# Input loads as one sequence on one queue, and the bias sums moved between tile transposes

## The chip, the cores and the metric

The kernel runs on one core of a Trainium2 chip. A core has five engines that run side by side, each through its own list of instructions: TensorE (PE in the profile; its weight loads are listed as PEld), VectorE (DVE), ScalarE (ACT), GpSimd (POOL) and SyncE (SP). They wait for each other through semaphores. SP, ACT and POOL also issue transfers (DMAs), each on its own queue, which 16 DMA engines carry out. The metric is the device time of the program in microseconds (us), as the median of several runs.

## The reference

The kernel computes six cross layers of a recommendation model, all in bf16, with a batch of 4096 rows and a width of 26 x 16 = 416 columns:

```python
x = x0                                # 4096 x 416
for l in range(6):
    x = x0 * (x @ ws[l] + bs[l]) + x  # ws[l]: 416 x 416, bs[l]: 416
return x
```

## The kernel before

The activations are held transposed, with features on the 128 partitions and batch rows along the free axis. The 416 features are three blocks of 128 (NC = 3) and a tail of 32. The batch is worked on in four strips of 1024 rows, and each strip in two halves of 512. The sum over the layers stays in PSUM, the memory that matmuls write: a bank is never cleared between the layers of a strip, so it holds the sum of all the products so far. Adding the sums of the biases so far and multiplying by x0 then gives the next layer's input. These bias sums are themselves a matmul: `bsa_sb` holds a row of ones and the six bias rows, `u_sb` is a triangle of ones, and the product lands in bank 1 and is copied to `cb_sb`.

Most matmuls are "column tiles": four of them (`tile_mm`, line 265), each with a 128 x 32 weight, write four groups of 32 partitions side by side. We call four such matmuls a group. The tail rows of the weights (`wt_sb`, `wc_sb`) are used by matmuls of 32 weight rows and 128 columns (lines 393 and 409).

**Steady work.** In layer n, PE does the first half's three output blocks (36 matmuls), then the tail rows, then the tail columns (12 matmuls) and the second half (36). When the tail rows are done (semaphore `s_ti`), DVE works through six `scalar_tensor_tensor` operations (line 537), three for each half; the next layer's tail rows wait for the last of them (`s_xb`). ACT and POOL handle the 32 tail features.

**The start.** Before anything else, PE runs 40 fill matmuls on a constant (line 130), whose results are not used. Rows 0-767 of the first strip are loaded as they are (`xin_sb`: rows 256-511, 0-255 and 512-767 are three transfers of 208 KB) and transposed on PE. Rows 768-1023 come by a DMA transpose (line 158), which SP issues after rows 0-255 have landed. W0 is the first layer's main weight, 312 KB. `xtl_sb` is the tail of rows 768-1023, read in pieces of 64 bytes.

PE's order is: the fill; the bias sums (16 matmuls, weights of 7 rows); four more fill matmuls; the transposes of rows 256-511 and then of rows 0-255, each as six full 128 x 128 transposes (line 312); then the first layer. Its first half is computed block by block of the inner dimension (k = 0, 1, 2). Inside k = 2, PE waits for rows 512-767 and xtl, and does the tail inputs and `third_input`, which transposes rows 512-767 as ordinary column-tile matmuls with an identity. The second half waits for the DMA transpose (`pe.wait_ge(s_x0T[0], 16)`, line 422).

DVE first copies the bias sums (line 506) and then the transposed blocks c = 0 and 2 to SBUF (line 512), while ACT copies c = 1 (line 561). The first matmul of the first layer waits for W0 and for three DVE copies (`s_inD`). The copies of the third input are on lines 517 (DVE) and 578 (ACT); line 576 is ACT's copy of the tail inputs. The order of everything is written out by hand.

Of the kernel before, what the change touches and what calls it, by code (L numbers as in the profile page):

```python
# [11 lines left out]
def bass_standalone__dcn_v2_cross__recsys_kernel(  # L12
# [20 lines left out]
    with ExitStack() as es:  # L33
        def sb(name, shape, dt=BF16):
            return es.enter_context(nc.sbuf_tensor(name, shape, dt))
# [20 lines left out]
        ones_sb = sb("ones_sb", [128, 256])  # L56
        bsa_sb = sb("bsa_sb", [L + 1, D])
        u_sb = sb("u_sb", [L + 1, L])
        cb_sb = sb("cb_sb", [128, NC + 1, L], FP32)
# [31 lines left out]
        def wmain(l):  # L91
            return ws[l, 0:DF, :].rearrange("(k p) n -> p k n", p=128)
# [35 lines left out]

        for q in range(4 * 10):
            nc.tensor.matmul(  # L130
                ps[lane(q % 4), 7, 0:256], lhsT=CONST[:, 0:32], rhs=CONST, start=True, stop=True,
                skip_group_check=True, tile_position=(0, 32 * (q % 4)),
            )
        nc.sync.dma_start(bsa_sb[1:L + 1, :], bs[:, :]).then_inc(s_bs, 16)
        nc.sync.dma_start(xin_sb[:, 0:2, :], x0_w[:, 0, :, :]).then_inc(s_xin[0], 16)
        nc.sync.dma_start(xin_sb[:, 4:6, :], x0_w[:, 2, :, :]).then_inc(s_xin[2], 16)
        nc.scalar.dma_start(xin_sb[:, 2:4, :], x0_w[:, 1, :, :]).then_inc(s_xin[1], 16)  # L137
        nc.scalar.dma_start(w_sb[:, 0, :, :], wmain(0)).then_inc(s_w[0], 16)
        nc.scalar.dma_start(xtl_sb[:, :, :], x0_v[:, 6:JS, DF:D]).then_inc(s_xtl0, 16)
        nc.gpsimd.memset(ones_sb[:, :], 1.0).then_inc(s_ones, 1)  # L140
        nc.vector.memset(wc_sb[:, :, :], 0.0).then_inc(s_zero, 1)
        nc.vector.memset(bsa_sb[0:1, :], 1.0).then_inc(s_zero, 1)

# [59 lines left out]
        def _(pool):  # L203
            def load_wc(i, g):
# [10 lines left out]
            pool.affine_select(  # L215
                out=u_sb[:, :], in_=ones_sb[0:L + 1, 0:L], pattern=[[1, L]],
                compare_op=ALU.is_ge, fill=0.0, base=1, channel_multiplier=-1,
            ).then_inc(s_set, 1)
            for g in (0, 2):
                load_wt(pool, g, 0, 1, s_wtp)  # L220
            pool.wait_ge(s_zero, 1)
            for i in range(2):
# [40 lines left out]
        def _(pe):  # L263
            def tile_mm(dst, lhsT, rhs, q, start):
                return pe.matmul(  # L265
                    dst, lhsT=lhsT, rhs=rhs, start=start, stop=True,
                    skip_group_check=True, tile_position=(0, 32 * q),
                )

            def fill(n):  # L270
                for i in range(n):
                    for q in range(4):
                        tile_mm(ps[lane(q), 7, 0:256], CONST[:, 0:32], CONST, q, True)

# [9 lines left out]
            def third_input():  # L284
                pe.wait_ge(s_inD, 4)
                for c in range(NC):
                    for j in range(2):
                        for q in range(4):
                            f0 = c * 128 + 32 * q
                            ins = tile_mm(  # L290
                                ps[lane(q), THIRD[c], j * 128:j * 128 + 128], xin_sb[:, 4 + j, f0:f0 + 32], ident[:, :], q, True
                            )
                    ins.then_inc(s_inT, 1)
# [10 lines left out]

            bias_sums()
            fill(1)
            pe.wait_ge(s_set, 1)
            for i, (h, c) in enumerate(IN_ORDER):
                if c == 0:
                    pe.wait_ge(s_xin[h], 16)  # L310
                for j in range(2 * h, 2 * h + 2):
                    ins = pe.transpose(
                        out=psT[:, IN_BANKS[h][c], (j % 2) * 128:(j % 2 + 1) * 128],
                        in_=xin_sb[:, j, c * 128:(c + 1) * 128], identity=ident[:, :],
                    )
                ins.then_inc(s_inT, 1)
# [187 lines left out]
        def _(dve):  # L504
            dve.wait_ge(s_cbp, 1)
            dve.tensor_copy(
                out=cb_sb[:, :, :], in_=ps[:, 1, 0:8 * (NC + 1)].rearrange("p (c e) -> p c e", e=8)[:, :, 0:L],
            ).then_inc(s_cb, 1)
            for i, (h, c) in enumerate(IN_ORDER):
                if c != 1:  # L510
                    dve.wait_ge(s_inT, i + 1)
                    dve.tensor_copy(
                        out=x0T_sb[:, c, h * 256:(h + 1) * 256], in_=psT[:, IN_BANKS[h][c], 0:256]
                    ).then_inc(s_inD, 1)
            for c in (0, 2):
                dve.wait_ge(s_inT, 2 * NC + c + 1)
                dve.tensor_copy(out=x0T_sb[:, c, 512:768], in_=ps[:, THIRD[c], 0:G]).then_inc(s_inD, 1)
            dve.wait_ge(s_cb, 1)
# [37 lines left out]
        def _(act):  # L556
# [20 lines left out]
            act.wait_ge(s_inT, 2 * NC + 2)  # L577
            act.activation(out=x0T_sb[:, 1, 512:768], in_=ps[:, THIRD[1], 0:G], func=ACTF.Copy).then_inc(s_inA, 1)
            act.wait_ge(s_cb, 1)
# [79 lines left out]
```

## Time and profile before

| what | us |
|---|---|
| median of 6 runs | 128.28 |
| lowest and highest | 128.07, 129.05 |
| the profiled execution | 128.11 |
| its span | 126.9 |
| PE busy | 123.0 (97% of the span) |
| DVE busy | 99.8 (79%) |
| ACT busy | 67.5 (53%) |
| POOL busy | 24.0 (19%) |

The span is the time from the first instruction to the last as the profiler records it; the run's own time is 1.2 us longer. A line of the profile names the source line, the engine, the operation, and "out<-in" with the shapes. `SPq`, `ACTq` and `POOLq` are the issues of transfers by those engines, not the transfers themselves. A `const` in a matmul is the constant of the fill.

The ends of matmuls are modelled and overlap, so a busy PE is not a PE at its peak. A wait in brackets behind a group is the idle time of its engine just before it, and what ended that time.

### The profile page before, as it was taken

What the parts mean: (1) busy time and instruction counts of PE and PEld (TensorE: products, weight loads), DVE (VectorE), ACT (ScalarE), POOL (GpSimd) and SP (SyncE); (2) the same over time, 40 slices, a digit from 0 to 9 for tenths busy, and PEclk for the clock granted to TensorE, in tenths of its full rate; (3) what the DMA queues carried; (4) which work ended last, traced back from release to release, by engine and by line L of the source; (5) the groups of instructions that cost most, each with busy time, mean ns of one, the idle gap of its engine ahead of it and who ended that gap; (6) DMA issues with size and microseconds to landing.
All of it is one profiled execution on the core that took longest, in us unless ns stands there. A gap on an engine that the chain in (4) does not pass through costs nothing.

```text
span 126.9 us, 5323 instructions
## 1 busy us (share of the span) xinstructions
PE 123.0 (97%) x2410; PEld 62.2 (49%) x2410; DVE 99.8 (79%) x154; ACT 67.5 (53%) x146; POOL 24.0 (19%) x44
## 2 busy tenths in 40 slices
PE   7899999999999999999999999999999999999991
PEld 5554544444444445445445445445454454454660
DVE  2359779779779779789788797797797797797973
ACT  0646357377726456475744564574762573566830
POOL 7512202202102013012022023022021021120450
PEclk9999999999999999999999999999999999999999
DMA  3962599400009999700007689940008910530006
GB/s 114 258 144 60 135 280 225 111 0 0 5 3 125 164 140 214 273 4 5 5 0 142 132 161 218 376 123 0 5 0 47 192 40 0 169 105 5 0 31 243
DMA packets 31889, 13.49 MB, mean 106 GB/s; under 512 B 24950, under 2 KB 31868, under 8 KB 31868
## 3 DMA queue, kind: packets, MB, share of 16 engines
q1 hardware_dynamic: 30476, 12.12, 44.9%
q10 hardware_dynamic: 1200, 0.99, 2.5%
q8 instruction: 19, 0.31, 1.0%
q0 software_dynamic: 192, 0.06, 0.4%
q14 instruction: 2, 0.02, 0.0%
HBM read 3.86 MB, written 3.41 MB: 57 GB/s over the span
## 4 chain that ended last, share of the span: by engine, by line
PE 94%; DMA 3%; DVE 0%; ACTq 0%; issue 0%
PE ps L265 81%; PE ps L393 10%; DMA w_sb<-in_ws_dram 3%; PE ps L449 2%; PE ps L464 1%; DVE o_sb L550 0%; PE ps L488 0%; ACTq L137 0%; PE ps L409 0%; PE ps L494 0%
## 5 line engine op out<-in xcount | busy, mean ns | idle before, releaser
L537 DVE SCALAR_TENSOR_TENSOR xT_sb<-ps,cb_sb,x0T_sb 128x512 bf16<-128x512 f32 x120 | 81.0, 744 | 16.5 <-PE ps L393 16.4
L265 PE MATMUL ps<-xT_sb,w_sb 128*32 128x512 bf16 (+1 forms) x1596 | 84.2, 364 | 0.0
L265 PEld LDWEIGHTS ps<-xT_sb,w_sb 128*32 128x32 bf16 x1596 | 41.1, 97 | 37.1 <-issue 4.0
L566 ACT ACTIVATE xt_sb<-xt_sb 32x256 bf16<-32x256 bf16 x76 | 31.5, 414 | 15.7 <-POOL xt_sb L242 15.1
L595 ACT ACTIVATE t_sb<-ps,cb_sb 64x256 f32<-64x256 f32 x46 | 21.5, 468 | 31.3 <-PE ps L265 31.0
L242 POOL TENSOR_TENSOR xt_sb<-t_sb,x0t_sb 128x256 bf16<-128x256 f32 x20 | 13.4, 672 | 81.5 <-ACT t_sb L595 81.5
L265 PE MATMUL ps<-x0T_sb,w_sb 128*32 128x512 bf16 (+1 forms) x336 | 18.5, 365 | 0.4 <-DMA w_sb<-in_ws_dram 0.3
L537 DVE SCALAR_TENSOR_TENSOR xo_sb<-ps,cb_sb,x0T_sb 128x512 bf16<-128x512 f32 x18 | 12.1, 745 | 2.5 <-PE ps L393 2.5
L265 PEld LDWEIGHTS ps<-x0T_sb,w_sb 128*32 128x32 bf16 x336 | 8.6, 97 | 7.9 <-issue 0.6
L393 PE MATMUL ps<-xt_sb,wt_sb 32*128 32x512 bf16 x76 | 11.6, 380 | 0.0
L614 ACT ACTIVATE x0t_sb<-x_sb 32x512 bf16<-32x512 bf16 x12 | 7.5, 626 | 0.3
L409 PE MATMUL ps<-xt_sb,wt_sb 32*128 32x512 bf16 x38 | 7.4, 386 | 0.0
L393 PE MATMUL ps<-xt_sb,wc_sb 32*128 32x256 bf16 x76 | 7.3, 268 | 0.0
L393 PEld LDWEIGHTS ps<-xt_sb,wt_sb 32*128 32x128 bf16 x76 | 2.2, 92 | 8.1 <-DVE xT_sb L537 8.1
L393 PEld LDWEIGHTS ps<-xt_sb,wc_sb 32*128 32x128 bf16 x76 | 3.8, 94 | 2.2
L242 POOL TENSOR_TENSOR xot_sb<-t_sb,x0t_sb 128x256 bf16<-128x256 f32 x3 | 2.0, 672 | 12.6 <-ACT t_sb L595 12.6
L550 DVE SCALAR_TENSOR_TENSOR o_sb<-ps,x0n_sb 128x416 bf16<-128x416 f32 x6 | 3.3, 586 | 1.0 <-PE ps L494 0.9
L570 ACT ACTIVATE xo_sb<-ps,cq_sb 128x512 bf16<-128x512 f32 x5 | 3.3, 686 | 1.1 <-PE ps L393 1.1
L130 PE MATMUL ps<-const-bfloat16-1.0 128*32 128x256 bf16 x40 | 2.3, 418 | 0.8 <-PEq L644 0.8
L561 ACT ACT_TABLE_LOAD x1 | 1.3, 1283 | 3.3 <-issue 3.3
L449 PE MATMUL ps<-w_sb,xT_sb 128*128 128x416 bf16 x12 | 2.8, 341 | 0.0
L265 PE MATMUL ps<-w_sb,xT_sb 128*32 128x416 bf16 x48 | 2.6, 339 | 0.0
(52 smaller groups left out, 38.8 us busy)
## 6 DMA issues: line engine op xcount, KB each, us to landing
out_dram<-o_sb SPq DMA_DIRECT2D x2, 832.0 KB, 4.8
w_sb<-in_ws_dram SPq DMA_DIRECT2D x5, 312.0 KB, 3.9
x0n_sb<-in_x_dram SPq DMA_DIRECT2D x1, 832.0 KB, 5.4
out_dram<-o_sb SPq DMA_DIRECT2D x1, 624.0 KB, 3.7
out_dram<-o_sb SPq DMA_DIRECT2D x3, 208.0 KB, 2.0
xin_sb<-in_x_dram SPq DMA_DIRECT2D x2, 208.0 KB, 3.2
out_dram<-o_sb ACTq DMA_DIRECT2D x2, 208.0 KB, 2.0
w_sb<-in_ws_dram ACTq DMA_DIRECT2D x1, 312.0 KB, 3.7
```

Source lines behind the costliest of these rows:

```text
L130: nc.tensor.matmul(ps[lane(q % 4), 7, 0:256], lhsT=CONST[:, 0:32], rhs=CONST, start=True, stop=True, skip_group_check=True, tile_position= ...
L242: pool.tensor_tensor(out=dst, in0=t32_sb[:, n % 2, :], in1=x0t_sb[:, s, 0:G], op=ALU.mult).then_inc(s_xt, 1)
L265: return pe.matmul(dst, lhsT=lhsT, rhs=rhs, start=start, stop=True, skip_group_check=True, tile_position=(0, 32 * q),)
L393: return pe.matmul(dst, lhsT=lhsT, rhs=srct[lane(g), cols], start=l == 0 and start, stop=True, skip_group_check=True, tile_position=(32 * ...
L409: pe.matmul(ps[:, NC * h + 2, :], lhsT=wt_sb[lane(g), l, 0:128], rhs=srct[lane(g), :].rearrange("p (b r) -> p b r", b=2)[:, ::-1, :], star ...
L449: pe.matmul(ps[:, NAT_BANKS[t], 0:D], lhsT=xT_sb[:, (L - 1) % 2, k, rows], rhs=w_sb[:, L - 1, k, :], start=False, stop=True, skip_group_ch ...
L537: dve.scalar_tensor_tensor(out=dst, in0=ps[:, NC * half + c, :], scalar=cb_sb[:, c, l:l + 1], in1=x0T_sb[:, c, o:o + H], op0=ALU.add, op1= ...
L550: dve.scalar_tensor_tensor(out=o_sb[:, j0 + t, :], in0=ps[:, NAT_BANKS[t], 0:D], scalar=1.0, in1=x0n_sb[:, t, :], op0=ALU.add, op1=ALU.mul ...
L566: ins = act.activation(out=buf[lane(g), G:2 * G], in_=buf[lane(g ^ 1), 0:G], func=ACTF.Copy)
L570: act.activation(out=xo_sb[:, NS - 1, c, half * H:(half + 1) * H], in_=ps[:, NC * half + c, :], func=ACTF.Identity, bias=cq_sb[:, c:c + 1] ...
L595: ins = act.activation(out=t32_sb[HALVES[h], n % 2, :], in_=tail(h), func=ACTF.Identity, bias=cb_sb[HALVES[h], NC, l:l + 1],)
L614: ins = act.activation(out=x0t_sb[lane(g), s + 1, :].rearrange("p (b n) -> p b n", b=2), in_=src[:, ::-1, :] if g % 2 else src, func=ACTF. ...
```

## The change

The four large input loads move to SP's queue, in the order rows 256-511, rows 0-255, W0, rows 512-767. Before, rows 256-511 and W0 were on ACT's queue. The bias load moves from SP's queue to ACT's. There it waits for a memset, because `bsa_sb` now has 128 rows, which are first cleared and then get the row of ones; `u_sb` has 128 rows too. The memset of `wc_sb` now comes third, and POOL's wait for it counts to 3.

On PE, the fill has 48 matmuls instead of 40, and the four extra fill matmuls behind the bias sums are gone. All transposes of rows 0-767 are column-tile transposes of 32 columns each, and `third_input` writes bf16 instead of fp32. The bias sums are computed with 128 rows, between the transposes of rows 256-511 and those of rows 0-255. DVE's copy of the sums moves behind its first two copies.

```diff
-        bsa_sb = sb("bsa_sb", [L + 1, D])
-        u_sb = sb("u_sb", [L + 1, L])
+        bsa_sb = sb("bsa_sb", [128, D])
+        u_sb = sb("u_sb", [128, L])
...
-        for q in range(4 * 10):
+        for q in range(4 * 12):
...
-        nc.sync.dma_start(bsa_sb[1:L + 1, :], bs[:, :]).then_inc(s_bs, 16)
+        nc.sync.dma_start(xin_sb[:, 2:4, :], x0_w[:, 1, :, :]).then_inc(s_xin[1], 16)
         nc.sync.dma_start(xin_sb[:, 0:2, :], x0_w[:, 0, :, :]).then_inc(s_xin[0], 16)
+        nc.sync.dma_start(w_sb[:, 0, :, :], wmain(0)).then_inc(s_w[0], 16)
         nc.sync.dma_start(xin_sb[:, 4:6, :], x0_w[:, 2, :, :]).then_inc(s_xin[2], 16)
-        nc.scalar.dma_start(xin_sb[:, 2:4, :], x0_w[:, 1, :, :]).then_inc(s_xin[1], 16)
-        nc.scalar.dma_start(w_sb[:, 0, :, :], wmain(0)).then_inc(s_w[0], 16)
+        nc.scalar.wait_ge(s_zero, 1)
+        nc.scalar.dma_start(bsa_sb[1:L + 1, :], bs[:, :]).then_inc(s_bs, 16)
         nc.scalar.dma_start(xtl_sb[:, :, :], x0_v[:, 6:JS, DF:D]).then_inc(s_xtl0, 16)
         nc.gpsimd.memset(ones_sb[:, :], 1.0).then_inc(s_ones, 1)
+        nc.vector.memset(bsa_sb[:, :], 0.0).then_inc(s_zero, 1)
+        nc.vector.wait_ge(s_zero, 1)
+        nc.vector.memset(bsa_sb[0:1, :], 1.0).then_inc(s_zero, 1)
         nc.vector.memset(wc_sb[:, :, :], 0.0).then_inc(s_zero, 1)
-        nc.vector.memset(bsa_sb[0:1, :], 1.0).then_inc(s_zero, 1)
...
-                out=u_sb[:, :], in_=ones_sb[0:L + 1, 0:L], pattern=[[1, L]],
+                out=u_sb[:, :], in_=ones_sb[:, 0:L], pattern=[[1, L]],
...
-            pool.wait_ge(s_zero, 1)
+            pool.wait_ge(s_zero, 3)
...
-            def fill(n):
-                for i in range(n):
-                    for q in range(4):
-                        tile_mm(ps[lane(q), 7, 0:256], CONST[:, 0:32], CONST, q, True)
+            def tile_tp(dst, src, q):
+                return pe.transpose(out=dst, in_=src, identity=ident[:, :], tile_position=(0, 32 * q))
...
-                            ins = tile_mm(
-                                ps[lane(q), THIRD[c], j * 128:j * 128 + 128], xin_sb[:, 4 + j, f0:f0 + 32], ident[:, :], q, True
+                            ins = tile_tp(
+                                psT[lane(q), THIRD[c], j * 128:j * 128 + 128], xin_sb[:, 4 + j, f0:f0 + 32], q
                             )
...
-            bias_sums()
-            fill(1)
             pe.wait_ge(s_set, 1)
             for i, (h, c) in enumerate(IN_ORDER):
+                if i == NC:
+                    bias_sums()
                 if c == 0:
                     pe.wait_ge(s_xin[h], 16)
-                for j in range(2 * h, 2 * h + 2):
-                    ins = pe.transpose(
-                        out=psT[:, IN_BANKS[h][c], (j % 2) * 128:(j % 2 + 1) * 128],
-                        in_=xin_sb[:, j, c * 128:(c + 1) * 128], identity=ident[:, :],
-                    )
+                for j in range(2):
+                    for q in range(4):
+                        f0 = c * 128 + 32 * q
+                        ins = tile_tp(
+                            psT[lane(q), IN_BANKS[h][c], j * 128:j * 128 + 128], xin_sb[:, 2 * h + j, f0:f0 + 32], q
+                        )
                 ins.then_inc(s_inT, 1)
...
-            dve.wait_ge(s_cbp, 1)
-            dve.tensor_copy(
-                out=cb_sb[:, :, :], in_=ps[:, 1, 0:8 * (NC + 1)].rearrange("p (c e) -> p c e", e=8)[:, :, 0:L],
-            ).then_inc(s_cb, 1)
             for i, (h, c) in enumerate(IN_ORDER):
+                if i == NC:
+                    dve.wait_ge(s_cbp, 1)
+                    dve.tensor_copy(
+                        out=cb_sb[:, :, :], in_=ps[:, 1, 0:8 * (NC + 1)].rearrange("p (c e) -> p c e", e=8)[:, :, 0:L],
+                    ).then_inc(s_cb, 1)
...
-                dve.tensor_copy(out=x0T_sb[:, c, 512:768], in_=ps[:, THIRD[c], 0:G]).then_inc(s_inD, 1)
+                dve.tensor_copy(out=x0T_sb[:, c, 512:768], in_=psT[:, THIRD[c], 0:G]).then_inc(s_inD, 1)
...
-            act.activation(out=x0T_sb[:, 1, 512:768], in_=ps[:, THIRD[1], 0:G], func=ACTF.Copy).then_inc(s_inA, 1)
+            act.activation(out=x0T_sb[:, 1, 512:768], in_=psT[:, THIRD[1], 0:G], func=ACTF.Copy).then_inc(s_inA, 1)
```

## The prediction

> **What bounds the kernel now.** I read the chain of waits first, in order of time. In this list, a line is start, length and what ran (us).
>
> ```profile
> 1.22 3.67 DMA w_sb<-in_ws_dram
> 4.94 2.80 PE ps L265 x76
> 7.74 0.36 PE ps L393
> 8.44 4.40 PE ps L265 x84
> 12.83 0.32 PE ps L393
> 13.38 4.33 PE ps L265 x84
> ```
>
> After the load of W0, TensorE (PE) is on the chain nearly to the end, and the pieces repeat every 4.87 us (13.38, 18.25, 23.12 and on). The edits lie ahead of the second layer, so the question is when that beat starts. The timeline of the first 14 us shows it; a bracket is the idle time before a group and what ended it.
>
> ```profile
> 0.83 2.33 PE L130 MATMUL ps<-const-bfloat16-1.0 128*32 128x256 bf16 x40 [0.83 <-PEq L644]
> ...
> 1.22 0.48 ACTq L138 DMA_DIRECT2D w_sb<-in_ws_dram  x1
> 1.25 0.37 SPq L135 DMA_DIRECT2D xin_sb<-in_x_dram  x1
> ...
> 3.63 0.98 PE L312 MATMUL ps<-ident,xin_sb 128*128 128x128 bf16 x12
> 3.88 1.28 SPq L158 DMA_TRANSPOSE x0T_sb<-in_x_dram  x1
> 4.06 0.93 DVE L512 COPY x0T_sb<-ps 128x256 bf16<-128x256 bf16 x4 [0.44 <-PE ps L312]
> ...
> 4.93 1.21 PEld L265 LDWEIGHTS ps<-x0T_sb,w_sb 128*32 128x32 bf16 x28 [0.50 <-DMA w_sb<-in_ws_dram]
> ...
> 7.13 0.76 DVE L517 CAST x0T_sb<-ps 128x256 bf16<-128x256 f32 x2 [2.13 <-PE ps L265]
> ...
> 8.43 1.96 PEld L265 LDWEIGHTS ps<-x0T_sb,w_sb 128*32 128x32 bf16 x48 [0.31 <-DMA x0T_sb<-in_x_dram]
> ...
> 8.55 4.04 DVE L537 SCALAR_TENSOR_TENSOR xT_sb<-ps,cb_sb,x0T_sb 128x512 bf16<-128x512 f32 x6 [0.67 <-PE ps L393]
> ```
>
> Three gates are to be seen: W0 at 4.9, the first tail rows (L393, 7.7 to 8.4), and the DMA transpose of rows 768-1023 at 8.43. The DMA view of the first 9 us gives the time from issue to landing (last column).
>
> ```profile
> w_sb<-in_ws_dram ACTq DMA_DIRECT2D x1, 312.0 KB, 3.7
> ...
> xin_sb<-in_x_dram ACTq DMA_DIRECT2D x1, 208.0 KB, 2.5
> ...
> xtl_sb<-in_x_dram ACTq DMA_DIRECT2D x1, 16.0 KB, 4.7
> x0T_sb<-in_x_dram SPq DMA_TRANSPOSE x1, 4.5
> ```
>
> Added to the issue times, rows 256-511 land at 3.3, rows 0-255 (2.6 after 1.25) at 3.85, W0 at 4.89, rows 512-767 (3.8 after 1.67) at 5.5, xtl at 6.44, the transpose at 8.4. Over two queues they land in the order in which their issues ended (1.19, 1.62, 1.70, 2.08, 2.25). The DMA engines' share is 0.86, 1.06 and 1.13 in the third, fourth and fifth us: they are full.
>
> **Part by part.**
> *The sequence on SP's queue.* The new order is the order of service that the landings already show, through engines that are already full. Four issues by the rows seen (0.40, 0.37, 0.48, 0.41) and gaps of about 0.05 end at 1.2, 1.6, 2.15 and 2.6; W0's, 0.45 later than before, still ends long before rows 0-255 have landed. So I take no shift for any of the four. Bounds for W0: 0.3 earlier, if bsa in front cost the first transfer its start (no row shows that), to 0.55 later, if xtl gets in front and takes as long as 208 KB do (3.3 to 3.85). Of 16 KB I expect far less; the value stays 0. SP's next wait is for rows 0-255, as before, and behind it stand the transpose, W1 and four wt loads, which keep their places.
>
> *ACT's queue* loses two issues (0.39, 0.48) and gains a wait for the first memset and the bsa issue (0.40). VectorE's (DVE's) first memset starts at 0.97 and takes between 0.2 and 0.46 (half of, or all of, the 0.41 and 0.46 of L142 and L141), so bsa is issued at 1.2 to 1.45 and ends by 1.85. xtl then ends by 2.4 (2.25 before), the two wt issues by 3.4 (3.24), and the table load, 1.28, by 4.7 (4.55). ACT's copies of the second k step are wanted at 5.6 and end at 5.22 now, so 0.15 is hidden. POOL's new count on s_zero is full after memsets of 0.41 and 0.46 more, at 2.3, and POOL gets there at 2.84: nothing.
>
> *Warm-up and transposes.* The 40 fills are 10 groups of four, (2.33-0.42)/9 = 0.21 apart; two more move the end of the streaming to 3.4, when rows 256-511 are there (3.3). Forty column-tile matmuls of 128 columns ran from 6.56 to 7.11, 0.055 a group. While fills take 0.21 for 256 columns (418 ns each, against 272 later), a group takes twice that. So the first 24 tile transposes run 3.4 to 4.0, the bias sums, 16 matmuls with 0.27 busy and 0.16 of it the last one's own time, to 4.15, and the second 24 follow at 0.055, with the first pair's result out at 4.42 (0.22 each). Padding to 128 rows and 128 partitions changes no count and no columns: nothing.
>
> DVE has five operations in place of four here: the copy of the sums (0.18) now stands between them. The copy of (0,0), third of the four, is started after 4.42 and the 0.18, at about 4.58, and ends at 4.87; it ended at 4.80 before. The first layer needs it and W0 (4.89). Value 0, bounds -0.05 to +0.15; its cover is W0, and without it the price is the 0.07.
>
> *xtl.* Seven groups of 0.216 from 4.94 are through at 6.45; the tail transposes came at 6.56, behind xtl's 6.44. Its queue no longer holds W0 in front, so it lands earlier: -0.1, bounds -0.1 and 0.
>
> *Third input in bf16.* Two DVE copies at 0.29 instead of 0.42 end about 0.25 earlier. Beside them ACT copies x0t (0.60 from 7.03) and c = 1 (0.38, to 7.90), unchanged in size, and DVE ended at 7.89. So only about 0.03 comes through. The next gate is wc: POOL's issues at 2.84 and 3.33 land 4.2 to 4.4 later, by 7.75, which allows a start 0.2 earlier.
>
> *Sum to the end of the first tail rows:* 0 - 0.10 - 0.03 = -0.13, so DVE starts at 8.42 instead of 8.55.
>
> *The transpose* waits for rows 0-255 (3.85), stands behind rows 512-767 in the queue as before, and lands at 8.4. Bounds: -0.25 (rows 0-255 come as early as W0's bound allows) to +0.4 (its first step is pushed back by W0 and rows 512-767 in one queue; between 3.88 and 8.4 nothing shows which part waits). Value 0. Then PE's next half starts at 8.43 as now, and its 36 matmuls before the next tail rows (2.12 from 10.72, less the last one's 0.38, plus 0.22) leave the array at 12.68. Those rows start at 12.76, 0.17 after DVE's 12.59. With DVE 0.13 earlier they could start at 12.63, but PE is free at 12.68: the gain is 0.08. From there on the beat of 4.87 holds, and the end moves by the same.
>
> **Sum:** 128.11 - 0.08 = 128.0 for the profiled execution, whose span is 126.9 with 1.2 around it. That execution lies 0.17 under the median of 128.28, so in the median I predict 128.2.
>
> *A rule against a trace.* The rows above: W0 was issued on ACT's queue 0.03 ahead of rows 0-255 on SP's, and landed 1.04 behind them. The Trainium skill ("DMA: Bandwidth & Descriptors", Queues, rings and completion order) says that an engine takes turns between queues, packet by packet. By that rule bsa could not get stuck behind W0, and the third rival below would drop out; the sum would be the same. The measured order decides here, so I keep that rival.
>
> *A rule against the change.* The first fills take 418 ns and the column matmuls of L265 364 on average, so the array speeds up while this stage runs, though the granted clock reads 1.00. The Trainium skill ("TensorE: Matmul & The Clock Gate", Part 4) says that transposes do not count as activity for the clock. By it, 72 transposes where there were 12 could keep the array slow; the twelve here ran while it sped up (315 ns the slowest, 219 the fastest), so I set this low.
>
> **The rivals.**
> 1. *Everything lands earlier* (chance 0.17). For it: without bsa ahead, the first transfer starts sooner. Against it: the engines are full. With the transfers 0.25 earlier, the transpose lands at 8.15 and no longer holds PE, but the (0,0) copy (4.87) holds the first layer. Left are the 0.13, and up to 0.1 more at the tail rows: 127.95 to 128.1.
> 2. *The transpose lands later* (0.15). By +0.2 to +0.4, less the 0.08 of room, the end moves by +0.1 to +0.3: 128.4 to 128.6.
> 3. *bsa lands behind W0, the other side* (0.14). PE stands in order: the sums now come ahead of the second 24 transposes. It costs nothing until bsa lands after 4.0. If its issue (1.6 to 1.85) is served behind W0 (issue ended 2.15), it lands near 4.9; sums to 5.05, the first pair out at 5.3, the copies by 5.75: the first layer starts 0.8 late, less the 0.13: +0.7, 129.0. For it: all small loads of ACT took over 4 us. Against it: 5 KB issued 0.3 ahead of W0.
> 4. *The array stays slow* (0.04): the seven groups before 6.45 at twice 0.216 are +1.5: 129.7.
>
> **How the numbers follow.** My forecast has 0.50: transfers keep their places, 128.2 with its own range of 128.0 to 128.4. About 0.5% (0.64 us) is what a measurement of this kernel can tell from no change, so the first two rivals lie inside it too. Slower: most of the third, and the fourth, 0.17. Faster needs 127.64 or less, beyond the first rival's end; for what I have not seen, 0.11. Same: 0.72. The range reaches from the first rival's end less the spread of the runs shown under their median (0.2), and some room, to the third rival's time: 127.6 to 129.0.
>
> **What would show it.** Right: W0 still ends the idle time before the first L265 work at 4.9; the tail inputs start at 6.45; L517 becomes a bf16 copy of 0.29; the first L537 starts at 8.4; the work at 8.4 is still released by the transpose. Wrong: an idle PE released by bsa near 4.9, the transpose landing away from 8.4, or matmuls of 512 columns 0.43 apart after 4.9.

## The result, and the profile after

The changed kernel is slower: 129.75 us in the median (128.68 to 131.51, 24 runs) against 128.47 for the kernel before (50 runs), and the ratio of the two is 1.0069 (95% interval 1.0051 to 1.0087). Its 24 runs lie in two groups, 13 of them at 128.7 to 129.8 (median 129.38) and 11 at 130.8 to 131.5, and the ratio leaves the upper group out. The profiled execution took 129.29 us, with a span of 128.1; so the two profiled executions are 1.18 us apart.

The chain of waits of the changed kernel, in order of time (start, length, what ran):

```profile
0.80 0.39 SPq L134
...
1.25 0.42 SPq L135
...
1.72 4.57 DMA w_sb<-in_ws_dram
...
6.33 1.92 PE ps L268 x44
8.25 0.33 PE ps L274 x24
8.58 0.43 PE ps L268 x8
...
9.02 0.37 PE ps L395
...
9.70 4.33 PE ps L268 x84
14.02 0.32 PE ps L395
...
14.57 4.33 PE ps L268 x84
```

The shape is the old one, with W0 at its head. But W0 is issued at 1.72 instead of 1.22, and takes 4.57 us instead of 3.67: it lands at 6.29 instead of 4.89. The beat of 4.87 us behind it is unchanged (9.70, 14.57). The timeline of the same execution shows the gates (a bracket is the idle time before a group and what ended it):

```profile
1.17 0.57 ACTq L139 DMA_DIRECT2D bsa_sb<-in_bs_dram  x1
...
1.72 0.43 SPq L136 DMA_DIRECT2D w_sb<-in_ws_dram  x1
1.78 0.44 ACTq L140 DMA_DIRECT2D xtl_sb<-in_x_dram  x1
...
3.42 0.83 PE L274 MATMUL ps<-ident,xin_sb 128*32 128x128 bf16 x24
...
4.62 0.72 DVE L515 COPY x0T_sb<-ps 128x256 bf16<-128x256 bf16 x2
...
6.33 1.69 PE L268 MATMUL ps<-x0T_sb,w_sb 128*32 128x512 bf16 x28 [1.33 <-DMA w_sb<-in_ws_dram]
...
8.42 0.51 DVE L520 COPY x0T_sb<-ps 128x256 bf16<-128x256 bf16 x2 [3.08 <-PE ps L274]
...
9.62 2.45 PE L268 MATMUL ps<-x0T_sb,w_sb 128*32 128x256 bf16 x48
...
9.84 0.75 DVE L540 SCALAR_TENSOR_TENSOR xT_sb<-ps,cb_sb,x0T_sb 128x512 bf16<-128x512 f32 x1 [0.92 <-PE ps L395]
```

TensorE (PE) stands idle for 1.33 us until W0 is there. From gate to gate, after less before:

| point | before | after | difference |
|---|---|---|---|
| W0 lands | 4.89 | 6.29 | +1.40 |
| first matmul of the first layer | 4.94 | 6.33 | +1.39 |
| first tail rows | 7.74 | 9.02 | +1.28 |
| first matmul behind the tail rows | 8.44 | 9.62 | +1.18 |
| a beat later | 13.38 | 14.57 | +1.19 |

(The chain gives 9.70 for the fourth point, because it counts from the end of the tail rows; the timeline has the first matmul at 9.62.) The 0.11 between the second and third rows is the wait for xtl that is gone: after, the tail inputs follow the first layer's matmuls without a gap. The 0.10 between the third and fourth is the wait for the DMA transpose, which is gone too: it lands at 8.96, before PE wants it at 9.62. So in these two profiles the whole loss is W0's landing, less about 0.2 us from the two waits.

### The profile page after: what moved, and what is told of

It reads as the page before. It is cut to its first block, busy times and chain, and to the rows that moved or that the text cites. A ratio compares the mean times of both kernels' runs of the same rounds, so it can differ in the third digit from the quotient of the medians.

```text
span 128.1 us, 5404 instructions
## 1 busy us (share of the span) xinstructions
PE 123.3 (96%) x2450; PEld 62.7 (49%) x2450; DVE 99.8 (78%) x155; ACT 67.5 (53%) x146; POOL 24.1 (19%) x44
## 3 DMA queue, kind: packets, MB, share of 16 engines
HBM read 3.86 MB, written 3.41 MB: 57 GB/s over the span
## 4 chain that ended last, share of the span: by engine, by line
PE 93%; DMA 4%; SPq 1%; DVE 0%; issue 0%
PE ps L268 80%; PE ps L395 10%; DMA w_sb<-in_ws_dram 4%; PE ps L451 2%; PE ps L466 1%; DVE o_sb L553 0%; PE ps L490 0%; SPq L135 0%; SPq L134 0%; PE ps L274 0%; PE ps L411 0%; PE ps L496 0%
## 5 line engine op out<-in xcount | busy, mean ns | idle before, releaser
L520 DVE COPY x0T_sb<-ps 128x256 bf16<-128x256 bf16 x2 | 0.5, 292 | 3.1 <-PE ps L274 3.1
```

## The experiments

First the two halves of the change by themselves, then W0's lateness, then TensorE's clock, then what the tensor side costs. All ratios are to runs of the kernel before on the same chip.

**The halves.** The first kernel is the kernel before with the queue moves alone:

```diff
-        nc.sync.dma_start(bsa_sb[1:L + 1, :], bs[:, :]).then_inc(s_bs, 16)
+        nc.sync.dma_start(xin_sb[:, 2:4, :], x0_w[:, 1, :, :]).then_inc(s_xin[1], 16)
         nc.sync.dma_start(xin_sb[:, 0:2, :], x0_w[:, 0, :, :]).then_inc(s_xin[0], 16)
+        nc.sync.dma_start(w_sb[:, 0, :, :], wmain(0)).then_inc(s_w[0], 16)
         nc.sync.dma_start(xin_sb[:, 4:6, :], x0_w[:, 2, :, :]).then_inc(s_xin[2], 16)
-        nc.scalar.dma_start(xin_sb[:, 2:4, :], x0_w[:, 1, :, :]).then_inc(s_xin[1], 16)
-        nc.scalar.dma_start(w_sb[:, 0, :, :], wmain(0)).then_inc(s_w[0], 16)
+        nc.scalar.dma_start(bsa_sb[1:L + 1, :], bs[:, :]).then_inc(s_bs, 16)
```

> The kernel before with the queue part alone: rows 256-511, rows 0-255, W0 and rows 512-767 on SyncE's queue, the bias load on ScalarE's queue (without the memset wait, since the bias tile keeps its 7 rows); TensorE's order is that of before. Theory M (mixing: xtl's 64-byte pieces on ScalarE's queue no longer stand behind W0 and are served beside it, so W0 lands late): W0 lands at 5.5 or later, the time is 129.0 to 130.0. Theory Q (one queue by itself carries the loads more slowly): the same numbers. Theory P (the loss comes from TensorE's side, the tile transposes or the bias sums between them): W0 lands near 4.9, the time stays within 0.3 of before.

The second has the changed order on TensorE and VectorE (48 fills, the column-tile transposes, the bias sums between them, bf16 for the third input), the old queues, and the bias block still with 7 rows:

```diff
-        for q in range(4 * 10):
+        for q in range(4 * 12):
...
-            bias_sums()
-            fill(1)
...
+                if i == NC:
+                    bias_sums()
```

> The changed kernel with the queues of before (bias load first on SyncE's queue, rows 256-511 and W0 on ScalarE's; the bias tile has 7 rows again, so that its load waits for no memset). Theories M and Q: W0 lands near 4.9 and the time is that of before or up to 0.2 less, since xtl is again behind W0 and the first tail rows start about 0.1 earlier. Theory P: 129.0 or more.

Measured: the queues alone 130.62 us, 1.0150 (1.0091 to 1.0209); W0 lands at 6.14. The tensor side alone 129.16, 1.0052 (1.0025 to 1.0080); W0 lands at 4.79. So the queue moves alone make W0 late, and the tensor side, which the prediction had at nothing, has a cost of its own. In the profile of the changed kernel that second cost lies hidden behind W0. The queues alone gave 129.31 in one run and 130.5 to 131.1 in the three others, much like the changed kernel's two groups; the ratio 1.0150 takes in both.

**Why W0 is late.** The bound in the prediction came from xtl, whose 64-byte pieces are issued on the other queue 0.06 us behind W0. The next kernel is the changed one with xtl's load moved behind all of the large ones:

```diff
         nc.sync.dma_start(xin_sb[:, 4:6, :], x0_w[:, 2, :, :]).then_inc(s_xin[2], 16)
+        nc.sync.dma_start(xtl_sb[:, :, :], x0_v[:, 6:JS, DF:D]).then_inc(s_xtl0, 16)
...
-        nc.scalar.dma_start(xtl_sb[:, :, :], x0_v[:, 6:JS, DF:D]).then_inc(s_xtl0, 16)
```

> The changed kernel with one edit: xtl is issued on SyncE's queue behind rows 512-767 instead of on ScalarE's behind the bias load. Theory M: the engines carry W0 undisturbed again, it lands at 4.8 to 5.1, and the time is 128.2 to 128.6. Theory Q: W0 lands as in the changed kernel, at 5.5 or later, 129.3 or more. Theory P: 129.3 or more with W0 near 4.9.

W0 landed at 6.20, and the time was 129.57 (1.0108, 1.0053 to 1.0162). xtl is not the cause. Next, the changed kernel with W0 on ScalarE's queue, behind the bias block's load, which waits for a memset:

```diff
-        nc.sync.dma_start(w_sb[:, 0, :, :], wmain(0)).then_inc(s_w[0], 16)
...
         nc.scalar.dma_start(bsa_sb[1:L + 1, :], bs[:, :]).then_inc(s_bs, 16)
+        nc.scalar.dma_start(w_sb[:, 0, :, :], wmain(0)).then_inc(s_w[0], 16)
```

> The changed kernel with one edit: W0 goes back to ScalarE's queue, behind the bias load and in front of xtl; rows 256-511, 0-255 and 512-767 stay on SyncE's. Theory M: xtl is behind W0 again, W0 lands at 4.8 to 5.2, the time is 128.2 to 128.7. Theory Q: two queues share the work again, the same numbers; the two are told apart by the kernel with xtl moved. Theory P: 129.3 or more.

131.68 us, 1.0244 (1.0216 to 1.0273): W0, issued at 1.79, landed at 7.17. It was off SyncE's queue and still late. What the late kernels share is the time of issue, so the next two part the time from the queue. In the kernel before, W0 stays on its queue and only waits for VectorE's two memsets:

```diff
         nc.scalar.dma_start(xin_sb[:, 2:4, :], x0_w[:, 1, :, :]).then_inc(s_xin[1], 16)
+        nc.scalar.wait_ge(s_zero, 2)
         nc.scalar.dma_start(w_sb[:, 0, :, :], wmain(0)).then_inc(s_w[0], 16)
```

> The kernel before with one edit: ScalarE waits for VectorE's two memsets before it issues W0, so W0 is issued near 1.9 instead of 1.22, on the same queue. The theory that xtl's pieces slow W0 has fallen (with xtl behind rows 512-767, W0 still landed at 6.2). Theory T (issue time: a transfer issued some 0.5 later is not prepared when the engines come to it, and starts at a trickle): W0 lands at 5.5 or later and the time is 129.0 or more. Theory Q (queue: W0 is late because it follows two transfers on its own queue): W0 lands at 4.9 to 5.2, the time is 128.3 to 128.8.

In the changed kernel, rows 256-511 go back to ScalarE's queue, so that W0 stays on SyncE's and is issued at 1.25:

```diff
-        nc.sync.dma_start(xin_sb[:, 2:4, :], x0_w[:, 1, :, :]).then_inc(s_xin[1], 16)
+        nc.scalar.dma_start(xin_sb[:, 2:4, :], x0_w[:, 1, :, :]).then_inc(s_xin[1], 16)
```

> The changed kernel with one edit: rows 256-511 go back to ScalarE's queue, in front of the wait and the bias load; SyncE issues rows 0-255 at 0.80 and W0 at 1.25. Theory T: W0 is issued early again and lands at 4.7 to 5.1, the time is 128.3 to 129.2. Theory Q: W0 still follows another transfer on its queue and lands at 5.5 or later, 129.2 or more.

Measured: the first 131.42 (1.0267, 1.0204 to 1.0330; four runs from 130.06 to 132.45, the profiled one 130.06), the second 129.73 (1.0107, 1.0036 to 1.0178; two runs near 129.0, the profiled one 128.88, and two near 130.4). The chain of waits of the kernel before with W0 held back:

```profile
1.89 5.06 DMA w_sb<-in_ws_dram
...
6.99 2.68 PE ps L266 x76
```

With its queue and its place on that queue unchanged, an issue 0.67 us later made W0 land 2.06 us later (6.95 instead of 4.89). (The issues behind it on ScalarE's queue move back with it, and rows 512-767, issued at 1.68 on the other queue, now come ahead of it.) And in the other kernel, on SyncE's queue but issued at 1.25, it landed at 4.99. So the queue by itself is not it. That second kernel still lost, at another place; the head of its chain is

```profile
1.86 5.39 DMA xtl_sb<-in_x_dram
```

so there xtl, issued 0.12 later than in the kernel before, landed at 7.25, 0.8 later. One thing was still tied to the time: a W0 issued late is also behind both loads of rows. The last test of this part starts from the tensor side with wide fills and the bias sums last (below) and exchanges two issues:

```diff
-        nc.sync.dma_start(bsa_sb[1:L + 1, :], bs[:, :]).then_inc(s_bs, 16)
         nc.sync.dma_start(xin_sb[:, 0:2, :], x0_w[:, 0, :, :]).then_inc(s_xin[0], 16)
+        nc.sync.dma_start(bsa_sb[1:L + 1, :], bs[:, :]).then_inc(s_bs, 16)
```

> The kernel of the tensor side with the wide fill and the bias sums last (128.66), with two issues on SyncE's queue exchanged: rows 0-255 at 0.80 us and the bias block behind them at 1.2. W0 keeps its issue at 1.22 on the scalar queue, but is now issued 0.4 behind rows 0-255 instead of 0.03 ahead of them: third of the large loads, as in the changed kernel. Theory T (the time of issue decides): W0 lands at 4.6 to 5.0, 127.9 to 128.6. Theory O (the place behind both loads of rows decides): W0 lands at 6.0 or later and 129.0 to 130.5.

128.73 us, 1.0012 (0.9986 to 1.0038). The DMA view of its first 9 us (time from issue to landing last) and its timeline:

```profile
w_sb<-in_ws_dram ACTq DMA_DIRECT2D x1, 312.0 KB, 3.7
```

```profile
0.80 0.40 SPq L134 DMA_DIRECT2D xin_sb<-in_x_dram  x1
0.80 0.40 ACTq L137 DMA_DIRECT2D xin_sb<-in_x_dram  x1
...
1.24 0.46 ACTq L138 DMA_DIRECT2D w_sb<-in_ws_dram  x1
```

Third of the large loads, but issued at 1.24, W0 landed at 4.98. Over all profiles taken:

| W0 issued | profiles | W0 lands |
|---|---|---|
| 0.80 (ScalarE's queue; the last kernel of this part) | 1 | 4.92 |
| 1.21 to 1.25 (either queue, second or third) | 12 | 4.70 to 4.99 |
| 1.71 to 1.89 (either queue) | 7 | 6.14 to 7.17 |

So the late landings go with the time of issue, on either queue. In five of the seven late profiles W0 was third on SyncE's queue and issued ahead of rows 512-767; in the other two it was on ScalarE's queue and behind them. Being third overall and being on SyncE's queue were each seen with a landing in time, and rows 512-767 can't be the cause in the five. No run has W0 third on one queue by 1.25, or issued late on ScalarE's queue with rows 512-767 behind it; so it is not ruled out that the five and the two have a reason each.

The table by stage shows where the time goes: busy time of PE, its weight loads, VectorE, ScalarE and GpSimd in each stretch, then the granted clock, the share of the 16 DMA engines and their GB/s. The kernel before, the changed one, the kernel before with W0 held back, and the last one:

```profile
3.00:4.00 1.00, 1.00 (x29) 0.67 (x26) 0.18 (x1) 0.73 (x1) 1.00 (x3) 1.00 1.06 369
4.00:5.00 1.00, 0.66 (x15) 0.50 (x16) 0.93 (x4) 0.99 (x3) 1.00 (x2) 1.00 1.13 347
```

```profile
3.00:4.00 1.00, 1.00 (x36) 0.71 (x32) 0.13 (x1) 0.76 (x1) 1.00 (x3) 1.00 0.89 257
4.00:5.00 1.00, 1.00 (x52) 0.73 (x40) 0.77 (x4) 0.99 (x3) 1.00 (x2) 1.00 1.03 311
```

```profile
3.00:4.00 1.00, 1.00 (x28) 0.67 (x25) 0.18 (x1) 0.16 (x1) 1.00 (x3) 1.00 0.84 200
4.00:5.00 1.00, 1.00 (x11) 0.82 (x8) 0.80 (x3) 1.00 (x1) 1.00 (x2) 1.00 0.76 218
```

```profile
3.00:4.00 1.00, 0.58 (x8) 0.00 (x0) 0.00 (x0) 0.74 (x1) 1.00 (x3) 1.00 1.05 371
4.00:5.00 1.00, 0.70 (x28) 0.73 (x32) 0.24 (x1) 0.57 (x2) 1.00 (x2) 1.00 1.11 364
```

From 3 to 5 us the engines move 716 KB before (369 and 347 KB), 568 after, 418 with W0 held back, and 735 in the last. In all seven profiles with a late W0 it is 418 to 597 KB, in the thirteen others 686 to 735. The packets of W0 say the same: a tenth of them has started by 3.44 before, and by 3.54 in the changed kernel. But from the first tenth to the last takes 0.7 us before, 1.4 after and 0.75 in the last run. So in the changed kernel the late issue hardly delays W0's start; W0 then runs at a lower rate. With W0 held back to 1.89 both happen: a tenth has started by 4.49, and the stretch takes 1.5 us. What lowers the rate inside the DMA engines these records don't show, and it stays open.

The opposite extreme was run as well: the changed kernel with W0 first of all on ScalarE's queue, and with the wide fills described below.

```diff
-        nc.sync.dma_start(w_sb[:, 0, :, :], wmain(0)).then_inc(s_w[0], 16)
         nc.sync.dma_start(xin_sb[:, 4:6, :], x0_w[:, 2, :, :]).then_inc(s_xin[2], 16)
+        nc.scalar.dma_start(w_sb[:, 0, :, :], wmain(0)).then_inc(s_w[0], 16)
         nc.scalar.wait_ge(s_zero, 1)
```

> The changed kernel with W0 as the first issue of the scalar queue, at 0.80 us, ahead of the wait of the bias block's load, rows 256-511, 0-255 and 512-767 on SyncE's at 0.80, 1.25 and 1.7, and the wide fill of 24 matmuls. Theory T: W0 lands by 4.9, 128.1 to 128.8, if rows 0-255 aren't later than 4.2 for it; they are the price, each 0.1 of theirs moves the transposes by as much. If one queue with the row loads in it is a loss of its own: 129.0 or more with W0 in time.

130.22 us, 1.0128 (1.0089 to 1.0167). W0 was in time (4.92), but its chain of waits begins with rows 0-255:

```profile
1.25 4.22 DMA xin_sb<-in_x_dram
...
5.49 4.86 DMA x0T_sb<-in_x_dram
```

Rows 0-255, issued at 1.25 as ever, land at 5.47 instead of 3.9. The price that the expectation named came out: the transposes, and the DMA transpose that waits for these rows (10.35), moved back with them. So an issue time of 1.25 does not by itself bring a load in on time: with W0 issued ahead of them, rows 0-255 landed 1.6 us later. And W0, issued 0.42 us earlier than in the kernel before, landed no earlier (4.92 against 4.89). In the opening about 370 GB/s are shared out (369 from 3 to 4 us in the kernel before, 381 from 4 to 5 us here), and the order of issue counts too.

**The upper group.** In the profiled execution above the granted clock was 1.00 throughout. A second profile of the unchanged after and before:

> The changed kernel as it is, a second profile. If the late W0 is a property of the kernel, W0 lands at 5.7 to 6.6 again; if it was an accident of the one execution, near 4.9. The time is 129.2 to 131.5.

> The kernel before as it is, a second profile: W0 lands near 4.9 and the DMA transpose near 8.4, the time is 128.0 to 129.0. If the transpose lands at 9 or later here too, its lateness in the changed kernel and in the kernel with TensorE's side alone is an accident, and no effect of the change.

They took 131.21 and 128.22 us. In the first, the table by stage has

```profile
6.00:7.00 1.00, 0.28 (x8) 0.18 (x12) 0.00 (x0) 0.00 (x0) 0.00 (x0) 1.00 1.47 123
7.00:8.00 1.00, 1.00 (x16) 0.39 (x12) 0.00 (x0) 0.00 (x0) 0.00 (x0) 0.58 0.71 142
8.00:9.00 1.00, 1.00 (x16) 0.48 (x12) 0.00 (x0) 0.00 (x0) 0.00 (x0) 0.50 0.92 279
9.00:10.00 1.00, 1.00 (x36) 0.74 (x32) 0.00 (x0) 0.00 (x0) 0.00 (x0) 0.50 0.22 28
10.00:11.00 1.00, 1.00 (x33) 0.53 (x22) 0.58 (x2) 0.87 (x2) 0.23 (x1) 0.72 0.00 0
```

The sixth figure after the comma is the granted clock: half from 7.15 to 10.57. The trace's clock records give the edges: up at 3.74, down at 7.15, up again at 10.57, in steps of 3.413 us. The W0-on-ScalarE kernel (131.68, profiled at 131.91) has the same picture: 3.89, 7.30, 10.71. In the changed kernel's first profile the clock came up at 5.24 and stayed. So the clock seems to be decided at edges one step apart, whose place differs from execution to execution (3.74 to 6.37 in the eleven profiles that recorded the first rise). Where an edge falls early, the step that follows holds the idle wait for W0: PE worked only about 1.3 us of the 3.41 between 3.74 and 7.15, and the next step ran at half clock. (On ScalarE's queue it was 0.8 us of the 3.41.) In the changed kernel's first profile the step from 5.24 has 2.3 us of work, and the clock stayed up. Half of 3.41 us is 1.7, which is about the distance between the two groups. The Trainium skill ("TensorE: Matmul & The Clock Gate", Part 1) describes such a free-running window of about 3.4 us and says that its phase makes runs differ; these runs agree. It puts the danger at idle gaps of more than about 3.4 us, and here one of 2.2 us was enough; the measurement decides.

That is two profiles. Of the 11 runs in the upper group, five have a mean granted clock of 0.985 to 0.987, which is what one half step gives (0.987 in the profile above). The six others read 0.998 to 1.00, so no half step is on record for them. The profiled execution of the queues alone (130.48) is such a case: its clock reads 1.00, with no record of an edge, but its first layer's groups lie 0.43 apart from 6.58 to 8.72 and half as far apart later. There the array seems to have come up late, near 8.9, instead of dropping once it was up. Whether the six are of that kind is not shown. The kernel before has three such high runs of 50, at 130.3 to 131.1, too.

To test it, 16 fill matmuls of 512 columns were put between the last transposes and the wait for W0 in the changed kernel:

```diff
+                        for i in range(4):
+                            for q in range(4):
+                                tile_mm(ps[lane(q), 2, :], CONST[:, 0:32], CONST, q, True)
```

> The changed kernel, with 16 matmuls of constants (512 columns, into a bank that is not yet used) between the last transposes and the wait for W0, some 0.9 us of work at the full clock, so that TensorE is not idle for 2 us there. Theory C (its executions near 131 us are those in which the clock drops to half after the idle time): none of them near 131, 129.0 to 129.7, the granted clock 0.9 or more from 7 to 11 us. Rival (the slow executions have another cause): executions near 131 as often as before, 129.2 to 131.5.

129.74 us (129.46 to 129.97), 1.0099 (1.0070 to 1.0128). None of its four runs is in the upper group, where the changed kernel had 11 of 24. By chance alone that would happen 9 times in 100, so it supports the theory without proving it. W0 landed at 6.87 in its profile, so the first loss stays; if the theory holds, the fill takes away the second.

**What the tensor side costs.** Its profile at 129.43 us showed two things: the first layer began at 5.39 with groups 0.43 apart (the clock came up at 6.37 only), and then PE waited for the DMA transpose until 9.71. In that transpose 21 packets took 1.27 to 1.78 us each and all ended near 7.9. In the same time, 6.16 to 7.14, a transfer of 16 KB on the instruction queue ran. Theory I was that this fetch stalls the transpose, and that TensorE reaches the place of the fetch sooner because it has 40 more matmuls ahead of the first layer. Three kernels test it: the kernel before with more and narrower fills, the tensor side with fewer and wider ones, and the latter with the bias sums last. (For fills of 512 columns the constant is made 512 wide.)

```diff
-        for q in range(4 * 10):
+        for q in range(4 * 20):
...
-                ps[lane(q % 4), 7, 0:256], lhsT=CONST[:, 0:32], rhs=CONST, start=True, stop=True,
+                ps[lane(q % 4), 7, 0:128], lhsT=CONST[:, 0:32], rhs=CONST[:, 0:128], start=True, stop=True,
```

> The kernel before, with the opening fill written as 80 matmuls of 128 columns in place of 40 of 256: the array's time for it is the same, TensorE has 40 more matmuls and 40 more weight loads ahead of the first layer, as the changed kernel has. Queues are those of before. Theory I (the DMA transpose of x0T stalls because TensorE reaches the end of its loaded instructions sooner, and their fetch, 16 KB on a queue of its own, falls into the transpose): the fetch comes near 5.3 to 6.2 us instead of 6.8 to 8.0, x0T lands at 9.0 us or later instead of 7.9 to 8.4, and the time is 128.6 to 129.5. Rival A (the fetch has nothing to do with it): x0T at 7.9 to 8.5 and 128.0 to 128.6, wherever the fetch lies.

```diff
-        for q in range(4 * 12):
+        for q in range(4 * 6):
...
-                ps[lane(q % 4), 7, 0:256], lhsT=CONST[:, 0:32], rhs=CONST, start=True, stop=True,
+                ps[lane(q % 4), 7, 0:512], lhsT=CONST[:, 0:32], rhs=CONST, start=True, stop=True,
```

> The kernel of the tensor side alone (129.16), with its fill as 24 matmuls of 512 columns in place of 48 of 256: the same time on the array, 24 matmuls and 24 weight loads fewer ahead of the first layer. Theory I: the fetch comes at 6.6 us or later, x0T lands by 8.6 us instead of 9.7, 128.1 to 128.6. Rival A: x0T at 9.0 to 9.7 and about 129.2, as without the edit.

```diff
-                if i == NC:
-                    bias_sums()
...
+            bias_sums()
             for s in range(NS):
```

> As the run with the fewer fills, with the bias sums behind both groups of transposes, and the first tail copy of the bias block accordingly ahead of the last of the transposed tiles' copies, so that the tile that the first layer reads first is copied sooner. If the bias sums between the transposes cost what the tensor side alone showed (its first layer began at 5.36 us, 5.13 in the kernel before), the first layer begins 0.1 to 0.3 us earlier than in the run with the fewer fills, and with theory I the time is 127.8 to 128.4. If the order of these sums is worth nothing, the two runs agree within 0.3 us.

More fills in the kernel before: 128.73 (1.0021, 0.9993 to 1.0049). Fewer and wider fills on the tensor side: 128.42 (0.9998, 0.9978 to 1.0017). Bias sums last: 128.66 (1.0022, 1.0000 to 1.0044). So the wider fills took the loss away, but theory I's place for the fetch failed: with 40 more matmuls it came at 6.93, as late as in the kernel before (6.81 and 8.02). And with no packet hung, x0T landed at 8.96 there, which neither side of the test had expected. The order of the bias sums moved the first layer by 0.13 (5.12 instead of 5.25) and nothing in the time.

Four more runs: the tensor side again, the same with 20 fills of 512 columns and 28 of 64 (as many instructions as the 48), the kernel before with 20 fills of 512, and the kernel with rows 256-511 back on ScalarE's queue with wide fills.

> The kernel of the tensor side alone once more, beside the next runs on one chip. If its 129.16 (1.0052) was its own, it comes out at 128.8 to 129.5, above the run with the fewer and wider fills (128.42) by 0.4 to 1.0 us. If the gap between the two was chance of the chip and the hour, it comes out at 128.2 to 128.7.

```diff
+            f = 512 if q < 4 * 5 else 64
...
+                ps[lane(q % 4), 7, 0:f], lhsT=CONST[:, 0:32], rhs=CONST[:, 0:f], start=True, stop=True,
```

> The tensor side alone with its fill as 20 matmuls of 512 columns and 28 of 64: as many instructions as in the run of the tensor side alone (48), the array's time about that of the wide fill (20 of 512 and 28 of 64 in place of 24 of 512). Theory I (the number of TensorE's instructions places the fetch, and that stalls x0T): x0T at 9 us or later and 128.9 to 129.5. Theory W (the wide matmuls bring the clock up sooner, the number of instructions is worth nothing): x0T by 8.6 us, full clock by 4.8 us, 128.2 to 128.6.

```diff
-        for q in range(4 * 10):
+        for q in range(4 * 5):
...
-                ps[lane(q % 4), 7, 0:256], lhsT=CONST[:, 0:32], rhs=CONST, start=True, stop=True,
+                ps[lane(q % 4), 7, 0:512], lhsT=CONST[:, 0:32], rhs=CONST, start=True, stop=True,
```

> The kernel before with its fill as 20 matmuls of 512 columns in place of 40 of 256, the same time on the array. Theory W: the full clock comes by 4.6 us in this profile (3.9 and 5.4 in the two of the kernel before), 127.9 to 128.2, and a narrower spread than 127.9 to 129.1. If the width of the fill is worth nothing here: 128.3 to 128.5.

```diff
-        nc.sync.dma_start(xin_sb[:, 2:4, :], x0_w[:, 1, :, :]).then_inc(s_xin[1], 16)
+        nc.scalar.dma_start(xin_sb[:, 2:4, :], x0_w[:, 1, :, :]).then_inc(s_xin[1], 16)
...
-        for q in range(4 * 12):
+        for q in range(4 * 6):
```

> The changed kernel with rows 256-511 back on the scalar queue, so that W0 is issued at 1.25 us on SyncE's, as in an earlier run (129.73), and with the fill as 24 matmuls of 512 columns in place of 48 of 256. If W0's time of issue and the opening's array time were all of the loss: 128.1 to 128.6. If the transfer of rows 768-799, issued at 1.86 us there and landed at 7.25, is a loss of its own: 128.8 to 129.5, with that transfer on the chain again.

The tensor side again: 129.16, 1.0049 (1.0019 to 1.0079), so its loss is its own. Mixed fills: 129.59, 1.0086 (1.0055 to 1.0117). Before with wide fills: 128.76, 0.9999 (0.9969 to 1.0029); width is worth nothing there. W0 at 1.25 with wide fills: 128.86, 1.0044 (1.0019 to 1.0069), with W0 at 4.70; xtl was not on its chain this time, which begins with rows 256-511 (landed at 3.88 instead of 3.3) and transposes at the slow rate.

The chains of waits of the tensor side's second profile, and of the one with wide fills:

```profile
3.97 5.43 DMA x0T_sb<-in_x_dram
...
9.44 4.40 PE ps L265 x84
```

```profile
7.94 0.36 PE ps L392
...
8.61 4.33 PE ps L265 x84
```

The first waits 5.43 us for the transpose and starts its beat at 9.44, the second never waits for it and starts at 8.61 (8.54 in its timeline), near the 8.44 of the kernel before. What the profiles have:

| kernel | fetch starts | long packets | x0T lands | clock up |
|---|---|---|---|---|
| tensor side | 6.16 | 21 | 9.71 | 6.37 |
| the same again | 5.85 | 19 | 9.40 | about 4.1 |
| 24 wide fills | 6.66 | 2 | 8.16 | 4.51 |
| the same, bias last | 6.75 | 0 | 8.28 | 4.63 |
| mixed fills | 6.64 | 0 | 8.99 | about 6.8 |
| after | 5.45 | 19 | 8.96 | 5.24 |
| before | 6.81 | 0 | 8.39 | 3.94 |
| before, again | 8.02 | 0 | 7.88 | 5.44 |
| before, more fills | 6.93 | 0 | 8.96 | about 6.4 |
| before, W0 held back | 8.98 | 11 | 9.29 | not seen |

(Long packets are those of the transpose that took over 0.45 us. "About" stands where no clock record exists: the time is read from where the matmuls become shorter. In the last row PE was idle from 5.08 to 6.99, with slow matmuls before and fast ones behind.) In all six profiles in which the fetch began before 6.2 us, 15 to 21 packets hung, and ended 0.8 to 0.95 us after the fetch did. In the eleven in which it began from 6.6 to 8.4 and W0 was in time, at most two did. In the three others W0 was late, the fetch began from 7.05 to 8.98, and 5 to 21 packets hung all the same; with W0 held back, the 11 had ended by 7.06, well before the fetch at 8.98. So packets can hang without the fetch, and the rest is an association: no run moved the fetch by itself, and with the mixed fills, as many instructions as on the tensor side gave a late fetch. In the one profile of the mixed fills no packet hung, and the array came up late (129.10, under their median of 129.59). So the tensor side's half per cent goes with two things in the profiles, a transpose that hangs and a late clock. How much of each a typical run has, and whether the fetch is the cause of the hanging, stays open. None of the versions beat the kernel before by more than can be measured.

## Why the prediction was wrong

The prediction was 128.2 (127.6 to 129.0), and the median came out at 129.75, the lower group alone at 129.38. *The sequence on SP's queue* is the step that failed. It gave W0's issue, 0.45 us later, the value 0, because it "still ends long before rows 0-255 have landed". The bound was +0.55. Measured: issued 0.50 later, +1.40 at the landing, +1.39 at the first layer. The sum had -0.08 for the profiled execution, and it was +1.18. The reasoning took the engines as full and the order of service as all that mattered; so a transfer could be issued at any time before its turn. The runs show that the time of issue itself counts: with W0 issued at 1.7 to 1.9 the engines move 418 to 597 KB from 3 to 5 us instead of 686 to 735. Even the one bound that reached to a loss had the wrong reason, xtl in front of W0; with xtl behind everything, W0 lands at 6.20. Among the signs that the prediction named, the landing of W0 at 6.3 instead of 4.9 is the one that told.

*bsa behind W0*, the rival on the other side, did not happen: bsa was issued at 1.17, with its issue done at 1.74, and landed at 3.13, long before W0. It even came ahead of rows 256-511 (3.28) and rows 0-255 (3.85), whose issues were done at 1.19 and 1.67. The rule that engines take turns between queues by packet (the Trainium skill, "DMA: Bandwidth & Descriptors", Queues, rings and completion order), which the prediction set aside there for the measured order, was the better guide for this small load. The forecast of that rival, 129.0, is near the lower group for another reason.

*The array stays slow* had 0.04 and a price of 1.5 us. A half clock in the first layer is on record in the second profile of the changed kernel (131.21), and five of the upper group's 11 runs have the mean clock that goes with it; the price is about 1.7 us. That this rival's number, 129.7, is near the median of all 24 runs is luck: that median is the upper edge of the lower group. The reason given, transposes that don't count as activity, does not fit that profile: the second 24 transposes ran there at 219 ns each, the full rate, and the clock fell at the end of the step in which PE waited for W0.

*Warm-up and transposes.* The copy of (0,0) ended at 4.91 (predicted 4.87), though by another way: the transposes ran at the slow rate to the end (24 in 0.83, predicted 0.6). "Its cover is W0, and without it the price is the 0.07": here the cover grew. With W0 in time the first layer began at 5.39 and 5.21 on the tensor side, 4.94 and 5.13 in the two profiles of the kernel before, so the price is nearer 0.1 to 0.45, with the clock's phase in it.

*The DMA transpose* had the value 0 and a bound of +0.4; it landed at 8.96, +0.57. It cost nothing in the changed kernel, because W0 had moved the point where it is wanted to 9.62. On the tensor side alone it landed at 9.4 to 9.7 and set the beat.

*ACT's queue, xtl, the third input* went as predicted where the time is concerned: nothing waits for ACT's later issues, the tail inputs follow at once (0.11 gained, 0.10 predicted), L520 is a bf16 copy of 0.29 us. Only xtl's landing was wrong: 7.39 instead of earlier than 6.44, unseen because the first layer is later still.

## What to carry to other kernels

In an opening like this one, with the DMA engines full, a load can't be issued at just any time before its turn: here issues 0.5 to 0.67 us later went with landings about 1.3 to 2.3 us later, on either queue. So lay out the issues of the opening by when each load is needed, and use two issuing engines so that the critical ones are all out early; one tidy sequence on one queue pushes its third member back by two issue times. And where the tensor engine waits in the first microseconds, look at more than one execution's clock: in two profiles here the same wait cost once more, at half clock.

## What the hardware showed that was not expected

- A load issued at 1.72 instead of 1.22 us started nearly as early (a tenth of its packets by 3.54 instead of 3.44) but took 1.4 instead of 0.7 us for the middle 80% of them.
- The clock of TensorE came up between 3.74 and 6.37 us after the start in the eleven profiles that recorded it, all of kernels that fill it from 0.83 on. In the two profiles in which it fell again in the opening it moved in steps of 3.413 us: PE had worked 1.3 and 0.8 us of one step, and the next ran at half clock.
- In the six profiles in which an instruction fetch of 16 KB ran during the first part of a DMA transpose, 15 to 21 of the transpose's packets took 0.46 to 1.78 us each and ended together. Three with a late W0 had 5 to 21 such packets with the fetch later.
